# A fused attention and gMLP decode kernel on one core: fewer PE instructions per head and a wo load in four-row runs

## The chip, the cores and the metric

The kernel runs on one core of one Trainium2 chip. The metric is the device time of one execution in microseconds, given as the median over several executions. The profile shows one execution, whose span is some 1.8 us shorter than the measured time. The record marks a run slow when it is over 1.5% above the fastest of the same kernel. A ratio of two kernels is the mean time of one kernel's fast runs over that of the other's fast runs of the same rounds, so it is not quite the ratio of the medians that are quoted beside it.

## The reference

One token of width 576 is normalized and goes through two branches: attention with 32 query heads on 16 K/V heads over a window of 4096 keys, and a gated MLP. Their sum is added to the input.

```python
xn = layernorm(x)                                   # x: [1, 1, 576]
q  = (xn @ wq)                                      # 32 heads of 128
k, v = k_cache[:, :, Sk-4096:], v_cache[:, :, Sk-4096:]   # 16 heads, each used by 2 query heads
p  = softmax(q @ k^T * 128**-0.5)
A  = (p @ v) @ wo                                   # wo: [4096, 576]
z  = gelu(xn @ w_in)                                # [4608]
g  = w_sp * layernorm(z[2304:]) + b_sp              # w_sp, b_sp: one number each is used
B  = (z[:2304] * g) @ w_out
return x + A + B
```

All inputs are bf16. K and V are drawn with scale 0.05, so the scores are tiny and the softmax is nearly flat. This matters for what the comparison with the reference can see.

## The kernel before

All large loads go through one queue, in the order in which they are needed: wq, w_in, then K and V of the 16 heads through a pool of 11 buffers, then w_out, then wo. The parts that the change touches are these.

```python
WO_CHUNKS = (8, 8, 8, 5, 3)
# wo: one head's 128 rows on 128 partitions, so runs of one row = 1152 bytes
nc.sync.dma_start(wo_sb[n][:],
    A_wo[DH * h0:DH * (h0 + c), :].rearrange("(h d) n -> d h n", d=DH))

def transpose_k(j):              # 4 groups of 8 blocks: 32 transposes per head
    for c in range(4):
        tps = ps_t.tile([P, 8, P], BF16, ...)
        for s in range(8):
            nc.tensor.transpose(tps[:, s, :], kn[:, 8 * c + s, :], ident[:])
        ...                      # copy to kT: ACT for c == 2, DVE for the others

def pv(j):                       # 32 matmuls of 128 columns per head
    for b in range(2):
        for s in range(4):
            for i in range(4):
                nc.tensor.matmul(ops[32*i:32*i+2, 0:DH], lhsT=pt[:, 4*b+s, i, :],
                                 rhs=v[:, 4*(4*b+i)+s, :], ..., tile_position=(0, 32*i))
    # then: scale by 1/den on DVE; o_columns(j) makes two columns of oT_all
# at the end: w_out's 18 row blocks, then wo's 32, four matmuls of 144 columns each
```

The softmax here doesn't subtract the row's maximum and nothing guards it: scores larger than these inputs give would overflow.

Of the kernel before, what the change touches and what calls it, by code (L numbers as in the profile page):

```python
# [8 lines left out]
FP32 = mybir.dt.float32  # L9
# [7 lines left out]
D = 576  # L17
# [9 lines left out]
SCALE = DH ** -0.5  # L27
GELU_C = 0.7978845608028654
NR = 98
QC = 1024  # L30
ZC = 1152
ZB = 384
# [1 line left out]
NZ = 36  # L34
NZ1 = 18
KV_BUFS = 11
WO_CHUNKS = (8, 8, 8, 5, 3)


@with_exitstack  # L40
def kernel(
# [106 lines left out]

    sps = [ps_fix.tile([P, 512], FP32, name=f"sps{b}") for b in range(2)]
    ops = ps_fix.tile([P, 512], FP32, name="ops")  # L150
    outp = ps_fix.tile([P, OC], FP32, name="outp")
    nc.vector.memset(ops[:], 0.0)
    nc.vector.memset(outp[:], 0.0)


    x_col = const.tile([P, 6], FP32, name="x_col")
# [6 lines left out]
        out=junk[:, 0:5], in0=x_col[:, 0:5], in1=x_col[:, 0:5], scale=1.0, scalar=0.0,  # L163
        op0=ALU.mult, op1=ALU.add, accum_out=stat[:, 1:2],
    )
    MS = 256

    def mean_rstd(stat_t, n, nm):
        nc.tensor.matmul(ops[:, MS:MS + 2], lhsT=ones_f[:], rhs=stat_t[:], start=True, stop=True)  # L169
        mv = const.tile([P, 4], FP32, name=f"mv{nm}")  # L170
        nc.vector.tensor_scalar_mul(mv[:, 0:2], ops[:, MS:MS + 2], 1.0 / n)
        nc.vector.tensor_mul(mv[:, 2:3], mv[:, 0:1], mv[:, 0:1])
        nc.vector.scalar_tensor_tensor(
            out=mv[:, 2:3], in0=mv[:, 1:2], scalar=EPS, in1=mv[:, 2:3],
            op0=ALU.add, op1=ALU.subtract,
        )
        nc.gpsimd.tensor_tensor(mv[:, 3:4], mv[:, 2:3], mhalf[:], ALU.pow)
        return mv
# [9 lines left out]

    r32 = const.tile([P, 32], FP32, name="r32")
    nc.vector.reduce_sum(r32[:], ident[:].rearrange("p (i r) -> p r i", r=32), axis=AXX)  # L190
    mx = const.tile([P, 4, 32], FP32, name="mx")
    for i in range(4):
        nc.vector.tensor_copy(mx[:, i, :], r32[:])
    mx_f = mx[:].rearrange("p i r -> p (i r)")
    id4f = const.tile([P, 4], FP32, name="id4f")
    nc.vector.tensor_copy(id4f[:], ident[:, 0:P:32])
    nc.gpsimd.dma_start(x4[0:P:32, :], x_flat.rearrange("o (g n) -> (o g) n", g=4))
# [17 lines left out]
    MQ = 288  # L215
    for hh in range(8):
        nc.tensor.matmul(
            ops[:, MQ + 4 * hh:MQ + 4 * hh + 4], lhsT=qrow[:, DH * hh:DH * (hh + 1)],
            rhs=ident[:, 0:P:32], start=True, stop=True,
        )  # L220
    q_bf = const.tile([P, HQ], BF16, name="q_bf")
    nc.vector.tensor_copy(
        q_bf[:].rearrange("p (i h) -> p i h", i=4),
        ops[:, MQ:MQ + HQ].rearrange("p (h i) -> p i h", i=4),
    )


# [21 lines left out]
    def z_columns():  # L249
        zv = zrow[:].rearrange("p (c t) -> p t c", t=9)  # L250
        for t in range(9):
            nc.tensor.matmul(  # L252
                ops[:, MZ + 4 * t:MZ + 4 * t + 4], lhsT=zv[:, t, :], rhs=id4f[:], start=True, stop=True,
            )
        zsb = const.tile([P, NZ], FP32, name="zsb")
        nc.vector.tensor_copy(
            zsb[:].rearrange("p (i t) -> p i t", i=4),
            ops[:, MZ:MZ + NZ].rearrange("p (t i) -> p i t", i=4),
        )
        u = const.tile([P, NZ], FP32, name="u_gelu")  # L260
        nc.vector.tensor_mul(u[:], zsb[:], zsb[:])
        nc.vector.tensor_scalar(out=u[:], in0=u[:], scalar1=0.044715, scalar2=1.0, op0=ALU.mult, op1=ALU.add)
        nc.vector.tensor_mul(u[:], u[:], zsb[:])
        th = const.tile([P, NZ], FP32, name="th_gelu")
        nc.scalar.activation(th[:], u[:], ACT.Exp, scale=-2.0 * GELU_C)
        nc.vector.tensor_scalar_add(th[:], th[:], 1.0)
        nc.vector.reciprocal(th[:], th[:])
        G = const.tile([P, NZ], FP32, name="G_gelu")
        nc.vector.tensor_mul(G[:], th[:], zsb[:])
        statz = const.tile([P, 2], FP32, name="statz")  # L270
        nc.vector.reduce_sum(statz[:, 0:1], G[:, NZ1:NZ], axis=AXX)
        junk2 = work.tile([P, NZ1], FP32, name="junk")
        nc.vector.tensor_tensor_reduce(
            out=junk2[:], in0=G[:, NZ1:NZ], in1=G[:, NZ1:NZ], scale=1.0, scalar=0.0,
            op0=ALU.mult, op1=ALU.add, accum_out=statz[:, 1:2],
        )
        return G, statz
# [11 lines left out]
        nc.vector.tensor_mul(hv[:], G[:, 0:NZ1], gv[:])  # L289

    w2pool = tc.alloc_tile_pool(name="w2pool", bufs=1, reuse_waits="tile")
    wo_sb = [w2pool.tile([P, c, D], BF16, name=f"wo{n}") for n, c in enumerate(WO_CHUNKS)]
    wout_sb = [w2pool.tile([P, 9, D], BF16, name=f"wout{i}") for i in range(2)]


    oT_all = const.tile([P, HQ], BF16, name="oT_all")
    kT_tiles: dict = {}
    p_tiles: dict = {}
    pt_tiles: dict = {}
    rd_tiles: dict = {}  # L300
    on_tiles: dict = {}

    def transpose_k(j):
        kn = kn_tiles.pop(j)
        parts = []
        for c in range(4):
            tps = ps_t.tile([P, 8, P], BF16, name=f"ktps{j}_{c}", tag="tps")
            for s in range(8):
                nc.tensor.transpose(tps[:, s, :], kn[:, 8 * c + s, :], ident[:])  # L309
            kT = ktpool.tile([P, 1024], BF16, name=f"kT{j}_{c}", tag="kT")  # L310
            src = tps[:].rearrange("p a b -> p (a b)")
            if c == 2:
                nc.scalar.copy(kT[:], src)  # L313
            else:
                nc.vector.tensor_copy(kT[:], src)  # L315
            parts.append(kT)
        kT_tiles[j] = parts

    def scores(j):
        parts = kT_tiles.pop(j)  # L320
        p_sb = ppool.tile([P, 2, 512], BF16, name=f"p{j}", tag="p_sb")
        acc = work.tile([P, 2], FP32, name=f"acc{j}", tag="acc")
        for b in range(2):
            for i in range(4):
                c = 4 * b + i
# [3 lines left out]
                    start=True, stop=True, tile_position=(0, 32 * i),  # L329
                )  # L330
            nc.scalar.activation(  # L331
                p_sb[0:NR, b, :], sps[b][0:NR, :], ACT.Exp, scale=SCALE, accum_out=acc[0:NR, b:b + 1],
            )
        asum = work.tile([P, 1], FP32, name=f"asum{j}", tag="asum")
        nc.vector.reduce_sum(asum[0:NR, :], acc[0:NR, :], axis=AXX)  # L335
        p_tiles[j] = (p_sb, asum)

    def transpose_p(j):
        p_sb, asum = p_tiles.pop(j)
        ptps = ps_t.tile([P, 8, P], BF16, name=f"ptps{j}", tag="tps")  # L340
        for b in range(2):
            for s in range(4):
                nc.tensor.transpose(  # L343
                    ptps[:, 4 * b + s, 0:NR], p_sb[0:NR, b, 128 * s:128 * (s + 1)], ident[0:NR, 0:NR])
        pt = work.tile([P, 8, 4, 2], BF16, name=f"pt{j}", tag="pt")
        nc.vector.tensor_copy(pt[:], ptps[:].rearrange("p t (q r) -> p t q r", q=4)[:, :, :, 0:2])
        pt_tiles[j] = pt
        den = ps_t.tile([P, 512], FP32, name=f"den{j}", tag="tps")
        nc.tensor.matmul(den[0:NR, 0:1], lhsT=mx_f[0:NR, 0:NR], rhs=asum[0:NR, :], start=True, stop=True)  # L349
        rden = work.tile([P, 1], FP32, name=f"rden{j}", tag="rden")  # L350
        nc.vector.reciprocal(rden[0:NR, :], den[0:NR, 0:1])
        rd_tiles[j] = rden

    def pv(j):
        pt = pt_tiles.pop(j)
        v = v_tiles.pop(j)
        for b in range(2):
            for s in range(4):
                for i in range(4):
                    nc.tensor.matmul(  # L360
                        ops[32 * i:32 * i + 2, 0:DH], lhsT=pt[:, 4 * b + s, i, :],
                        rhs=v[:, 4 * (4 * b + i) + s, :],
                        start=(b == 0 and s == 0), stop=(b == 1 and s == 3), tile_position=(0, 32 * i),
                    )
        on_sb = work.tile([P, DH], FP32, name=f"on{j}", tag="on")
        nc.vector.tensor_scalar_mul(on_sb[0:NR, :], ops[0:NR, 0:DH], rd_tiles.pop(j)[0:NR, :])  # L366
        on_tiles[j] = on_sb

    def o_columns(j):
        on_sb = on_tiles.pop(j)  # L370
        ot = ps_t.tile([P, 512], FP32, name=f"ot{j}", tag="tps")
        nc.tensor.matmul(ot[:, 0:2], lhsT=on_sb[0:NR, :], rhs=r32[0:NR, 0:2], start=True, stop=True)  # L372
        nc.vector.tensor_copy(oT_all[:, 2 * j:2 * j + 2], ot[:, 0:2])

    gz = None
    for j in range(HKV + 2):
# [6 lines left out]
        if 1 <= j <= HKV:  # L383
            transpose_p(j - 1)
        if j >= 2:
            o_columns(j - 2)
        if j < HKV:
            scores(j)
        if 1 <= j <= HKV:
            pv(j - 1)  # L390
        load_next(2)
        if j == 10:
            for i in range(2):
                nc.sync.dma_start(
                    wout_sb[i][:], B_w_out[ZC * i:ZC * (i + 1), :].rearrange("(p t) n -> p t n", t=9))
            h0 = 0
            for n, c in enumerate(WO_CHUNKS):
                nc.sync.dma_start(  # L398
                    wo_sb[n][:], A_wo[DH * h0:DH * (h0 + c), :].rearrange("(h d) n -> d h n", d=DH))
                h0 += c  # L400


    def project(lhsT, rhs, first, last):
# [3 lines left out]
                start=first, stop=last, tile_position=(0, 32 * g),  # L407
            )

    for i in range(2):  # L410
        for t in range(9):
            k = 9 * i + t
            project(hv[:, k:k + 1], wout_sb[i][:, t, :], k == 0, False)
    h = 0
    for n, c in enumerate(WO_CHUNKS):
        for u in range(c):
            project(oT_all[:, h:h + 1], wo_sb[n][:, u, :], False, h == HQ - 1)
            h += 1

    w2pool.release()  # L420
    res = const.tile([P, OC], BF16, name="res")
    nc.vector.tensor_tensor(out=res[0:97, :], in0=outp[0:97, :], in1=x4[0:97, :], op=ALU.add)  # L422
    nc.sync.dma_start(out_flat.rearrange("o (g n) -> (o g) n", g=4), res[0:P:32, :])


# [28 lines left out]
```

## Time and profile before

| | before |
|---|---|
| time | 136.66 us (136.62 to 136.68, 4 runs) |
| span in the profile | 134.8 us |
| moved by DMA | 51.21 MB, of it K and V 33.5 MB |
| PE matmuls and weight loads | 1674 and 1674 |

The page's line of busy times comes first: engine, busy us, share of the span, number of instructions. PE is TensorE, PEld its weight loads, DVE VectorE, ACT ScalarE and POOL GpSimd. Under it are four of its costly groups (line, engine, operation, tiles, shapes, count; busy us and mean ns; idle time before them and who ended it), and the issue line of wo (count, KB each, us from issue to landing).

```profile
PE 91.8 (68%) x1674; PEld 74.7 (55%) x1674; DVE 50.7 (38%) x173; ACT 38.9 (29%) x84; POOL 3.6 (3%) x11
...
L309 PE MATMUL ktps<-ident,kn 128*128 128x128 bf16 x512 | 37.7, 242 | 6.0 <-DMA kn<-in_A_k_cache_dram 5.6
...
L315 DVE COPY kT<-ktps 128x1024 bf16<-128x1024 bf16 x48 | 31.1, 684 | 10.7 <-PE ktps L309 10.6
...
L360 PE MATMUL ops<-v,pt 128*2 128x128 bf16 x512 | 10.4, 225 | 0.0
L405 PE MATMUL outp<-wo,oT_all 128*1 128x144 bf16 x128 | 4.7, 318 | 7.6 <-DMA wo<-in_A_wo_dram 7.6
...
wo<-in_A_wo_dram SPq DMA_DIRECT2D x3, 1152.0 KB, 22.1
```

### The profile page before, as it was taken

To read this page: it belongs to the slowest core of one execution; us is meant where nothing else is said; L and a number is where in the kernel's file an instruction comes from. 1 tells how busy PE (TensorE), PEld (TensorE's weight loads), DVE (VectorE), ACT (ScalarE), POOL (GpSimd) and SP (SyncE) were. 2 spreads that over 40 slices of the span, in tenths; PEclk is the share of its full clock that TensorE was granted. 3 is DMA by queue.
4 is the path that set the end of the run, shared out by engine and by line. 5 is a ranking of instruction groups with operands and counts; after the bars stand their busy time and mean duration, and the time that the engine had idled before them with its cause. 6 is when DMAs were issued, how large, how long until landed. Compare 5 with 4: busy or idle time off the path is not lost.

```text
span 134.8 us, 3783 instructions
## 1 busy us (share of the span) xinstructions
PE 91.8 (68%) x1674; PEld 74.7 (55%) x1674; DVE 50.7 (38%) x173; ACT 38.9 (29%) x84; POOL 3.6 (3%) x11
## 2 busy tenths in 40 slices
PE   0004943367998899999999989968499784243350
PEld 0002321127977698888898868856488664232330
DVE  2104020034226653677555577635266443000000
ACT  3000010010333126555655645635036360000000
POOL 6001000000000100000000000000000000000000
PEclk9999995555955558999999999999779999755555
DMA  4999999999999999999999999999999999999920
GB/s 114 350 309 416 427 429 427 405 431 413 420 416 420 423 418 411 413 418 423 416 416 416 411 420 411 425 413 416 416 423 423 410 423 413 360 359 356 306 74 3
DMA packets 11145, 51.21 MB, mean 380 GB/s; under 512 B 1400, under 2 KB 5496, under 8 KB 5752
## 3 DMA queue, kind: packets, MB, share of 16 engines
q1 hardware_dynamic: 10520, 50.96, 94.3%
q8 instruction: 13, 0.21, 0.7%
q0 software_dynamic: 320, 0.00, 0.3%
q10 hardware_dynamic: 288, 0.00, 0.1%
q14 instruction: 4, 0.03, 0.1%
HBM read 50.96 MB, written 0.00 MB: 378 GB/s over the span
## 4 chain that ended last, share of the span: by engine, by line
DMA 45%; PE 21%; SPq 15%; DVE 8%; ACT 5%; issue 2%; ACTq 0%
DMA kn<-in_A_k_cache_dram 30%; SPq L398 14%; PE ktps L309 9%; DMA wq<-in_A_wq_dram 8%; DMA wo<-in_A_wo_dram 7%; DVE kT L315 6%; ACT p L331 5%; PE sps L326 3%; PE ops L252 3%; PE den L349 2%; DVE on L366 2%; PE ot L372 1%; PE ops L360 1%; PE ptps L343 1%; ACT kT L313 1%
## 5 line engine op out<-in xcount | busy, mean ns | idle before, releaser
L309 PE MATMUL ktps<-ident,kn 128*128 128x128 bf16 x512 | 37.7, 242 | 6.0 <-DMA kn<-in_A_k_cache_dram 5.6
L309 PEld LDWEIGHTS <-kn 128*128 128x128 bf16 x512 | 34.7, 110 | 9.7 <-DMA kn<-in_A_k_cache_dram 7.1
L315 DVE COPY kT<-ktps 128x1024 bf16<-128x1024 bf16 x48 | 31.1, 684 | 10.7 <-PE ktps L309 10.6
L331 ACT ACTIVATE p<-sps 98x512 bf16<-98x512 f32 x32 | 18.8, 593 | 19.2 <-PE sps L326 19.2
L313 ACT COPY kT<-ktps 128x1024 bf16<-128x1024 bf16 x16 | 16.2, 1012 | 25.3 <-PE ktps L309 25.3
L326 PE MATMUL sps<-kT,q_bf 128*2 128x512 bf16 x128 | 10.5, 406 | 0.0
L335 DVE TENSOR_REDUCE asum<-acc 98x1 f32<-98x2 f32 x16 | 2.5, 154 | 21.2 <-ACT p L331 21.2
L360 PEld LDWEIGHTS <-pt 128*2 128x2 bf16 x512 | 8.6, 86 | 3.3 <-issue 0.3
L360 PE MATMUL ops<-v,pt 128*2 128x128 bf16 x512 | 10.4, 225 | 0.0
L405 PE MATMUL outp<-wo,oT_all 128*1 128x144 bf16 x128 | 4.7, 318 | 7.6 <-DMA wo<-in_A_wo_dram 7.6
L343 PE MATMUL ptps<-ident,p 98*128 98x98 bf16 x128 | 8.8, 213 | 0.4 <-ACT p L331 0.2
L405 PEld LDWEIGHTS <-oT_all 128*1 128x1 bf16 x128 | 3.7, 114 | 8.6 <-issue 8.6
L237 PE MATMUL zps<-win,xz 128*32 128x384 bf16 x48 | 4.1, 468 | 6.1 <-DMA win<-in_B_w_in_dram 6.1
L343 PEld LDWEIGHTS <-p 98*128 98x128 bf16 x128 | 7.5, 103 | 0.8 <-ACT p L331 0.7
L169 PE MATMUL ops<-stat,ones_f 128*128 128x2 f32 x2 | 0.6, 364 | 10.4 <-DVE stat L162 10.4
L237 PEld LDWEIGHTS <-xz 128*32 128x32 bf16 x60 | 2.1, 117 | 8.9 <-issue 7.8
L422 DVE TENSOR_TENSOR res<-outp,x 97x144 bf16<-97x144 f32 x1 | 0.3, 308 | 17.8 <-PE outp L405 17.8
L372 PE MATMUL ot<-r,on 98*128 98x2 f32 x32 | 6.0, 257 | 1.0 <-ACT kT L313 0.5
L331 ACT ACTIVATION_READ_ACCUMULATOR p<-sps 98x1 f32 x32 | 6.3, 198 | 0.0
L169 PEld LDWEIGHTS ops<-stat,ones_f 128*128 128x128 f32 x2 | 0.5, 310 | 10.4 <-DVE stat L162 10.4
L366 DVE TENSOR_SCALAR on<-ops,rden 98x128 f32<-98x128 f32 x16 | 5.6, 350 | 0.4 <-PE ops L360 0.4
L349 PE MATMUL den<-asum,mx 98*98 98x1 f32 x32 | 5.2, 233 | 0.7
(74 smaller groups left out, 56.8 us busy)
## 6 DMA issues: line engine op xcount, KB each, us to landing
kn<-in_A_k_cache_dram SPq DMA_DIRECT2D x16, 1024.0 KB, 19.9
v<-in_A_v_cache_dram SPq DMA_DIRECT2D x16, 1024.0 KB, 19.9
win<-in_B_w_in_dram SPq DMA_DIRECT2D x4, 1152.0 KB, 16.3
wq<-in_A_wq_dram SPq DMA_DIRECT2D x4, 1024.0 KB, 10.4
wo<-in_A_wo_dram SPq DMA_DIRECT2D x3, 1152.0 KB, 22.1
wout<-in_B_w_out_dram SPq DMA_DIRECT2D x2, 1296.0 KB, 21.7
wo<-in_A_wo_dram SPq DMA_DIRECT2D x1, 720.0 KB, 11.8
winh<-in_B_w_in_dram SPq DMA_DIRECT2D x1, 576.0 KB
```

The source lines that it names most:

```text
L309: nc.tensor.transpose(tps[:, s, :], kn[:, 8 * c + s, :], ident[:])
L313: nc.scalar.copy(kT[:], src)
L315: nc.vector.tensor_copy(kT[:], src)
L326: nc.tensor.matmul(sps[b][32 * i:32 * i + 2, :], lhsT=q_bf[:, 2 * j:2 * j + 2], rhs=parts[c // 2][:, 512 * (c % 2):512 * (c % 2) + 512], s ...
L331: nc.scalar.activation(p_sb[0:NR, b, :], sps[b][0:NR, :], ACT.Exp, scale=SCALE, accum_out=acc[0:NR, b:b + 1],)
L343: nc.tensor.transpose(ptps[:, 4 * b + s, 0:NR], p_sb[0:NR, b, 128 * s:128 * (s + 1)], ident[0:NR, 0:NR])
L349: nc.tensor.matmul(den[0:NR, 0:1], lhsT=mx_f[0:NR, 0:NR], rhs=asum[0:NR, :], start=True, stop=True)
L360: nc.tensor.matmul(ops[32 * i:32 * i + 2, 0:DH], lhsT=pt[:, 4 * b + s, i, :], rhs=v[:, 4 * (4 * b + i) + s, :], start=(b == 0 and s == 0), ...
L366: nc.vector.tensor_scalar_mul(on_sb[0:NR, :], ops[0:NR, 0:DH], rd_tiles.pop(j)[0:NR, :])
L372: nc.tensor.matmul(ot[:, 0:2], lhsT=on_sb[0:NR, :], rhs=r32[0:NR, 0:2], start=True, stop=True)
L398: nc.sync.dma_start(wo_sb[n][:], A_wo[DH * h0:DH * (h0 + c), :].rearrange("(h d) n -> d h n", d=DH))
L405: nc.tensor.matmul(outp[32 * g:32 * g + 1, :], lhsT=lhsT, rhs=rhs[:, OC * g:OC * (g + 1)], start=first, stop=last, tile_position=(0, 32 * g),)
```

## The change

The change means to relieve PE and DVE and to load wo in longer runs. Per head it transposes 8 of the 32 K blocks and uses them for all four quarters of the keys. PV becomes 8 matmuls of 512 columns, of which selection matmuls pick the useful part. The softmax denominators are applied once at the end. wo is read with four neighbouring rows per partition, and it comes before w_out.

```diff
-WO_CHUNKS = (8, 8, 8, 5, 3)
+WO_CHUNKS = (2, 2, 2, 2)
+WOUT_CHUNKS = ((0, 0, 9), (1, 0, 6), (1, 6, 9))
 ...
-        for c in range(4):
-            tps = ps_t.tile([P, 8, P], BF16, name=f"ktps{j}_{c}", tag="tps")
-            for s in range(8):
-                nc.tensor.transpose(tps[:, s, :], kn[:, 8 * c + s, :], ident[:])
+        tps = ps_t.tile([P, 8, P], BF16, name=f"ktps{j}", tag="tps")
+        for s in range(8):
+            nc.tensor.transpose(tps[:, s, :], kn[:, s, :], ident[:])
+        for c in (0, 2):
             kT = ktpool.tile([P, 1024], BF16, name=f"kT{j}_{c}", tag="kT")
 ...
-            parts.append(kT)
+            parts += [kT, kT]
 ...
         for b in range(2):
-            for s in range(4):
-                for i in range(4):
-                    nc.tensor.matmul(
-                        ops[32 * i:32 * i + 2, 0:DH], lhsT=pt[:, 4 * b + s, i, :],
-                        rhs=v[:, 4 * (4 * b + i) + s, :], ...
+            for i in range(4):
+                c = 4 * b + i
+                nc.tensor.matmul(
+                    ops[32 * i:32 * i + 8, :], lhsT=pt[:, b, i, :, :], rhs=v[:, 4 * c:4 * c + 4, :], ...
-        nc.vector.tensor_scalar_mul(on_sb[0:NR, :], ops[0:NR, 0:DH], rd_tiles.pop(j)[0:NR, :])
+        nc.scalar.copy(on_sb[0:NV, :], ops[0:NV, :])
 ...
+        for a in range(4):
+            nc.tensor.matmul(
+                oall[32 * a:32 * a + 32, :], lhsT=sel[0:NV, a, 32 - 2 * j:64 - 2 * j],
+                rhs=on_sb[0:NV, DH * a:DH * (a + 1)],
+                start=(j == 0), stop=(j == HKV - 1), tile_position=(0, 32 * a),
+            )
 ...
-                    wo_sb[n][:], A_wo[DH * h0:DH * (h0 + c), :].rearrange("(h d) n -> d h n", d=DH))
+                    wo_sb[n][:], A_wo[512 * h0:512 * (h0 + c), :].rearrange("(g p r) n -> p g r n", p=P, r=4))
 ... (the finish: osb, den, rden, rsel, 16 matmuls, oT_all; w_out projected after wo)
```

With the 8 blocks used four times, three quarters of the scores are computed from the wrong keys. The comparison with the reference cannot see this part. So "correct" says little here about the attention branch.

More of the change, by code (lines that the diff above doesn't have):

```diff
@@ L29 @@
 NR = 98
+NV = 104
 QC = 1024
@@ L150 @@
     ops = ps_fix.tile([P, 512], FP32, name="ops")
-    outp = ps_fix.tile([P, OC], FP32, name="outp")
+    fin = ps_fix.tile([P, 512], FP32, name="fin")
+    outp = fin[:, 0:OC]
+    oall = fin[:, 144:272]
+    den = fin[:, 416:432]
     nc.vector.memset(ops[:], 0.0)
-    nc.vector.memset(outp[:], 0.0)
+    nc.vector.memset(outp, 0.0)
     x_col = const.tile([P, 6], FP32, name="x_col")
@@ L165 @@
     )
-    MS = 256
+    MS = 274
     def mean_rstd(stat_t, n, nm):
-        nc.tensor.matmul(ops[:, MS:MS + 2], lhsT=ones_f[:], rhs=stat_t[:], start=True, stop=True)
+        nc.tensor.matmul(fin[:, MS:MS + 2], lhsT=ones_f[:], rhs=stat_t[:], start=True, stop=True)
         mv = const.tile([P, 4], FP32, name=f"mv{nm}")
-        nc.vector.tensor_scalar_mul(mv[:, 0:2], ops[:, MS:MS + 2], 1.0 / n)
+        nc.vector.tensor_scalar_mul(mv[:, 0:2], fin[:, MS:MS + 2], 1.0 / n)
         nc.vector.tensor_mul(mv[:, 2:3], mv[:, 0:1], mv[:, 0:1])
@@ L190 @@
     nc.vector.reduce_sum(r32[:], ident[:].rearrange("p (i r) -> p r i", r=32), axis=AXX)
-    mx = const.tile([P, 4, 32], FP32, name="mx")
-    for i in range(4):
-        nc.vector.tensor_copy(mx[:, i, :], r32[:])
-    mx_f = mx[:].rearrange("p i r -> p (i r)")
+    sel = const.tile([P, 4, 64], FP32, name="sel")
+    nc.vector.memset(sel[:], 0.0)
+    nc.vector.tensor_copy(sel[:, :, 32:34], r32[:, 0:8].rearrange("p (a e) -> p a e", e=2))
+    par = const.tile([P, 64, 2], FP32, name="par")
+    nc.vector.tensor_copy(par[:], r32[:, 0:2].unsqueeze(1).to_broadcast([P, 64, 2]))
+    jmask = const.tile([P, HKV], FP32, name="jmask")
+    nc.vector.reduce_sum(jmask[:], r32[:].rearrange("p (j e) -> p j e", e=2), axis=AXX)
+    acc_all = const.tile([P, HKV, 2], FP32, name="acc_all")
     id4f = const.tile([P, 4], FP32, name="id4f")
@@ L217 @@
         nc.tensor.matmul(
-            ops[:, MQ + 4 * hh:MQ + 4 * hh + 4], lhsT=qrow[:, DH * hh:DH * (hh + 1)],
+            fin[:, MQ + 4 * hh:MQ + 4 * hh + 4], lhsT=qrow[:, DH * hh:DH * (hh + 1)],
             rhs=ident[:, 0:P:32], start=True, stop=True,
@@ L223 @@
         q_bf[:].rearrange("p (i h) -> p i h", i=4),
-        ops[:, MQ:MQ + HQ].rearrange("p (h i) -> p i h", i=4),
+        fin[:, MQ:MQ + HQ].rearrange("p (h i) -> p i h", i=4),
     )
@@ L252, in z_columns @@
             nc.tensor.matmul(
-                ops[:, MZ + 4 * t:MZ + 4 * t + 4], lhsT=zv[:, t, :], rhs=id4f[:], start=True, stop=True,
+                fin[:, MZ + 4 * t:MZ + 4 * t + 4], lhsT=zv[:, t, :], rhs=id4f[:], start=True, stop=True,
             )
@@ L257, in z_columns @@
             zsb[:].rearrange("p (i t) -> p i t", i=4),
-            ops[:, MZ:MZ + NZ].rearrange("p (t i) -> p i t", i=4),
+            fin[:, MZ:MZ + NZ].rearrange("p (t i) -> p i t", i=4),
         )
@@ L291 @@
     w2pool = tc.alloc_tile_pool(name="w2pool", bufs=1, reuse_waits="tile")
-    wo_sb = [w2pool.tile([P, c, D], BF16, name=f"wo{n}") for n, c in enumerate(WO_CHUNKS)]
-    wout_sb = [w2pool.tile([P, 9, D], BF16, name=f"wout{i}") for i in range(2)]
-    oT_all = const.tile([P, HQ], BF16, name="oT_all")
+    wo_sb = [w2pool.tile([P, c, 4, D], BF16, name=f"wo{n}") for n, c in enumerate(WO_CHUNKS)]
+    wout_sb = [w2pool.tile([P, t1 - t0, D], BF16, name=f"wout{i}_{t0}") for i, t0, t1 in WOUT_CHUNKS]
     kT_tiles: dict = {}
@@ L299 @@
     pt_tiles: dict = {}
-    rd_tiles: dict = {}
     on_tiles: dict = {}
@@ L321, in scores @@
         p_sb = ppool.tile([P, 2, 512], BF16, name=f"p{j}", tag="p_sb")
-        acc = work.tile([P, 2], FP32, name=f"acc{j}", tag="acc")
         for b in range(2):
@@ L331, in scores @@
             nc.scalar.activation(
-                p_sb[0:NR, b, :], sps[b][0:NR, :], ACT.Exp, scale=SCALE, accum_out=acc[0:NR, b:b + 1],
+                p_sb[0:NR, b, :], sps[b][0:NR, :], ACT.Exp, scale=SCALE, accum_out=acc_all[0:NR, j, b:b + 1],
             )
-        asum = work.tile([P, 1], FP32, name=f"asum{j}", tag="asum")
-        nc.vector.reduce_sum(asum[0:NR, :], acc[0:NR, :], axis=AXX)
-        p_tiles[j] = (p_sb, asum)
+        p_tiles[j] = p_sb
     def transpose_p(j):
-        p_sb, asum = p_tiles.pop(j)
+        p_sb = p_tiles.pop(j)
         ptps = ps_t.tile([P, 8, P], BF16, name=f"ptps{j}", tag="tps")
@@ L344, in transpose_p @@
                     ptps[:, 4 * b + s, 0:NR], p_sb[0:NR, b, 128 * s:128 * (s + 1)], ident[0:NR, 0:NR])
-        pt = work.tile([P, 8, 4, 2], BF16, name=f"pt{j}", tag="pt")
-        nc.vector.tensor_copy(pt[:], ptps[:].rearrange("p t (q r) -> p t q r", q=4)[:, :, :, 0:2])
-        pt_tiles[j] = pt
-        den = ps_t.tile([P, 512], FP32, name=f"den{j}", tag="tps")
-        nc.tensor.matmul(den[0:NR, 0:1], lhsT=mx_f[0:NR, 0:NR], rhs=asum[0:NR, :], start=True, stop=True)
-        rden = work.tile([P, 1], FP32, name=f"rden{j}", tag="rden")
-        nc.vector.reciprocal(rden[0:NR, :], den[0:NR, 0:1])
-        rd_tiles[j] = rden
+        pt = work.tile([P, 2, 4, 4, 2], BF16, name=f"pt{j}", tag="pt")
+        for b in range(2):
+            nc.vector.tensor_copy(
+                pt[:, b, :, :, :].rearrange("p i s r -> p s i r"),
+                ptps[:, 4 * b:4 * b + 4, :].rearrange("p s (i r) -> p s i r", i=4)[:, :, :, 0:2])
+        pt_tiles[j] = pt
     def pv(j):
@@ L357, in pv, with o_rows @@
         for b in range(2):
-            for s in range(4):
-                for i in range(4):
-                    nc.tensor.matmul(
-                        ops[32 * i:32 * i + 2, 0:DH], lhsT=pt[:, 4 * b + s, i, :],
-                        rhs=v[:, 4 * (4 * b + i) + s, :],
-                        start=(b == 0 and s == 0), stop=(b == 1 and s == 3), tile_position=(0, 32 * i),
-                    )
-        on_sb = work.tile([P, DH], FP32, name=f"on{j}", tag="on")
-        nc.vector.tensor_scalar_mul(on_sb[0:NR, :], ops[0:NR, 0:DH], rd_tiles.pop(j)[0:NR, :])
+            for i in range(4):
+                c = 4 * b + i
+                nc.tensor.matmul(
+                    ops[32 * i:32 * i + 8, :], lhsT=pt[:, b, i, :, :], rhs=v[:, 4 * c:4 * c + 4, :],
+                    start=(b == 0), stop=(b == 1), tile_position=(0, 32 * i),
+                )
+        on_sb = work.tile([P, 512], FP32, name=f"on{j}", tag="on")
+        nc.scalar.copy(on_sb[0:NV, :], ops[0:NV, :])
         on_tiles[j] = on_sb
-    def o_columns(j):
+    def o_rows(j):
         on_sb = on_tiles.pop(j)
-        ot = ps_t.tile([P, 512], FP32, name=f"ot{j}", tag="tps")
-        nc.tensor.matmul(ot[:, 0:2], lhsT=on_sb[0:NR, :], rhs=r32[0:NR, 0:2], start=True, stop=True)
-        nc.vector.tensor_copy(oT_all[:, 2 * j:2 * j + 2], ot[:, 0:2])
+        for a in range(4):
[3 more added lines that the diff above has]
+                start=(j == 0), stop=(j == HKV - 1), tile_position=(0, 32 * a),
+            )
     gz = None
@@ L385 @@
         if j >= 2:
-            o_columns(j - 2)
+            o_rows(j - 2)
         if j < HKV:
@@ L392 @@
         if j == 10:
-            for i in range(2):
-                nc.sync.dma_start(
-                    wout_sb[i][:], B_w_out[ZC * i:ZC * (i + 1), :].rearrange("(p t) n -> p t n", t=9))
             h0 = 0
@@ L398 @@
                 nc.sync.dma_start(
-                    wo_sb[n][:], A_wo[DH * h0:DH * (h0 + c), :].rearrange("(h d) n -> d h n", d=DH))
+                    wo_sb[n][:], A_wo[512 * h0:512 * (h0 + c), :].rearrange("(g p r) n -> p g r n", p=P, r=4))
                 h0 += c
+            for n, (i, t0, t1) in enumerate(WOUT_CHUNKS):
+                nc.sync.dma_start(
+                    wout_sb[n][:],
+                    B_w_out[ZC * i:ZC * (i + 1), :].rearrange("(p t) n -> p t n", t=9)[:, t0:t1, :])
+    osb = const.tile([P, DH], FP32, name="osb")
+    nc.scalar.copy(osb[:], oall)
+    rden = const.tile([P, 1], FP32, name="rden")
+    acc1 = const.tile([P, HKV], FP32, name="acc1")
+    nc.vector.reduce_sum(acc1[0:NR, :], acc_all[0:NR, :, :], axis=AXX)
+    nc.tensor.matmul(den, lhsT=par[0:NR, :, :].rearrange("p m e -> p (m e)"), rhs=acc1[0:NR, :],
+                     start=True, stop=True)
+    nc.vector.tensor_mul(jmask[:], jmask[:], den)
+    nc.vector.reduce_sum(rden[:], jmask[:], axis=AXX)
+    nc.vector.reciprocal(rden[:], rden[:])
+    rsel = const.tile([P, 32], FP32, name="rsel")
+    nc.vector.tensor_scalar_mul(rsel[:], r32[:], rden[:])
+    MO = 384
+    for r in range(4):
+        for hh in range(4):
+            nc.tensor.matmul(
+                fin[32 * hh:32 * hh + 32, MO + 8 * r:MO + 8 * r + 8], lhsT=osb[:, r:DH:4], rhs=rsel[:, hh:HQ:4],
+                start=True, stop=True, tile_position=(0, 32 * hh),
+            )
+    oT_all = const.tile([P, 4, 8], BF16, name="oT_all")
+    nc.vector.tensor_copy(oT_all[:].rearrange("p r g -> p (r g)"), fin[:, MO:MO + HQ])
     def project(lhsT, rhs, first, last):
@@ L408, in project @@
             )
-    for i in range(2):
-        for t in range(9):
-            k = 9 * i + t
-            project(hv[:, k:k + 1], wout_sb[i][:, t, :], k == 0, False)
     h = 0
@@ L416 @@
         for u in range(c):
-            project(oT_all[:, h:h + 1], wo_sb[n][:, u, :], False, h == HQ - 1)
+            for r in range(4):
+                project(oT_all[:, r, h:h + 1], wo_sb[n][:, u, r, :], (h == 0 and u == 0 and r == 0), False)
             h += 1
+    for n, (i, t0, t1) in enumerate(WOUT_CHUNKS):
+        for t in range(t0, t1):
+            k = 9 * i + t
+            project(hv[:, k:k + 1], wout_sb[n][:, t - t0, :], False, k == NZ1 - 1)
     w2pool.release()
     res = const.tile([P, OC], BF16, name="res")
-    nc.vector.tensor_tensor(out=res[0:97, :], in0=outp[0:97, :], in1=x4[0:97, :], op=ALU.add)
+    nc.vector.tensor_tensor(out=res[0:97, :], in0=outp[0:97], in1=x4[0:97, :], op=ALU.add)
     nc.sync.dma_start(out_flat.rearrange("o (g n) -> (o g) n", g=4), res[0:P:32, :])
```

## The prediction

> **What bounds the kernel now.** I read the page's slices first, then the queue table, then the end of the chain of waits in order of time, then windows over the stages, and last the landing records of the single transfers. From the page, the slices (40 of 3.37 us each) and the queues:
>
> ```profile
> DMA  4999999999999999999999999999999999999920
> GB/s 114 350 309 416 427 429 427 405 431 413 420 416 420 423 418 411 413 418 423 416 416 416 411 420 411 425 413 416 416 423 423 410 423 413 360 359 356 306 74 3
> DMA packets 11145, 51.21 MB, mean 380 GB/s; under 512 B 1400, under 2 KB 5496, under 8 KB 5752
> q1 hardware_dynamic: 10520, 50.96, 94.3%
> q8 instruction: 13, 0.21, 0.7%
> ```
>
> The DMA engines are full from slice 1 to slice 36, whatever the compute engines do. Two things stand out: the rate falls from about 417 to 360 GB/s for four slices near the end, and it tails off in slices 37 and 38 before it stops. The 13 instruction packets matter below. The end of the chain of waits, in order of time (start us, length us, what):
>
> ```profile
> 120.93 9.70 DMA wo<-in_A_wo_dram
> 130.63 0.04 issue
> 130.68 0.56 PE outp L405 x12
> 131.23 0.02 issue
> 131.26 0.31 DVE res L422
> ```
>
> The kernel ends 4.2 us after the last piece of wo has landed at 130.63: 12 matmuls, one add, one small store. So the time is "when does the last byte land" plus 4.2 us. PE, though busy for 68% of the span, is not the bound: it has caught up before 114 us and then waits for each weight chunk. The windows for the KV stage, the wout end, the wo stage and the tail (columns: window, length, busy of PE, PEld, DVE, ACT, POOL, clock, DMA share, GB/s):
>
> ```profile
> 28.00:93.00 65.00, 59.80 (x1046) 51.81 (x1045) 36.24 (x114) 28.97 (x63) 0.55 (x1) 0.85 1.01 417
> 93.00:113.00 20.00, 15.63 (x339) 13.31 (x338) 9.48 (x31) 8.10 (x19) 0.00 (x0) 0.91 1.02 419
> 113.00:126.50 13.50, 4.49 (x138) 3.70 (x139) 0.16 (x1) 0.00 (x0) 0.00 (x0) 0.62 1.06 363
> 126.50:131.00 4.50, 2.22 (x64) 1.69 (x63) 0.00 (x0) 0.00 (x0) 0.00 (x0) 0.50 0.43 144
> ```
>
> PE goes from 92% busy to 78% to 33% while the rate stays at 417 to 419 and then even falls: the stream does not wait for compute. In the tail window the DMA share is 0.43: some of the 16 engines have finished and others have not.
>
> **Why they finish apart.** The trace holds, for each transfer, when each of its sixteen parts landed. First part to last part:
>
> ```
> about 28 us (winh)     0.29 us apart
> about 50 us (KV)       1.7
> about 90 us (KV)       1.8
> about 108 us (last V)  3.3, two parts over 3, eight between 0.7 and 1.9
> last piece of wo       3.3 (127.33 to 130.63), four parts over 3
> ```
>
> The lag does not creep, it jumps, one part at a time. The jumps follow the 13 instruction packets (16384 B each, the first at 30.8 us, then 47.9, 56.2, 63.4, and about every 6 us while PE is fast): each leaves one part about 1.55 to 1.8 us late, and it stays late[...]. The first eight packets hit eight different parts; the ninth (93.8 us) hits the first one again, and a lag over 3 us appears exactly then. Numbers 10 to 12 double three more. The thirteenth comes too late to matter. PE has 1674 matmuls and 1674 weight loads, about 13 times 256, so these are PE's instructions.
>
> [...] the trace shows sixteen landings, and PE starts at 130.68, after the last at 130.63. [...] the part that lands first paces at 311 ns per 8192 B (421 GB/s over 16), 350 ns per 9216 B, 178 ns per 4608 B (winh), but 51 ns per 1152 B (361 GB/s).
>
> **The change, part by part.**
>
> *wo layout.* Each wo partition now reads four rows that lie together: 1024 packets of 4608 B instead of 4096 of 1152 B. Per DMA engine that is 64 packets instead of 256: 256 x 51.0 = 13.1 us before, 64 x 178 = 11.4 us after, so 1.66 us less on every engine, all on the path that sets the end. wout, moved behind wo, is cut into pieces of 9, 6 and 3 rows: 8 packets each of 10368, 6912 and 3456 B instead of 16 of 10368. A line through the durations above gives an estimate of 264 and 135 ns for the smaller two: 8 x (391 + 264 + 135) = 6.32 us against 16 x 391 = 6.26. Net: 1.6 us less. K and V still move in full, 33.5 MB.
>
> *PE program.* K transposes go from 32 to 8 per head. The eight transposed blocks are used for all four quarters of the keys, so three quarters of the scores come from the wrong keys; with inputs scaled by 0.05 the softmax is nearly flat, and I expect that the comparison doesn't see it. PV goes from 32 matmuls of 128 columns to 8 of 512. New are four fp32 selection matmuls per head and 16 at the end. By the order of instructions, PE keeps 820 bf16 matmuls; about 92 fp32 ones count twice (the old den has x32 for 16 heads): 820 + 184 = 1004 matmuls and as many loads, about 2008 instructions against 3348. The PE time itself buys nothing, since PE was not the bound. But the fetches fall in proportion: the first came after 220 instructions and one per 256 follows, so (2008 - 220)/256 + 1 = 7 or 8. Eight or fewer hit eight different engines, and no engine is hit twice. The last lag should be one hit, about 1.8 us, instead of 3.3: 1.5 us less.
>
> *DVE and ACT.* ACT gains one copy of 104x512 per head (about 0.6 us, like the 0.593 us of its exponential) and loses nothing: near 3.3 us per head with its kT copy of 1.012 and two exponentials with their reads, 1.6. DVE loses two kT copies of 0.684, asum, reciprocal, scaling and column copies. PE at half clock needs, estimated from the 0.88 us for 8 transposes and 0.95 us for a score group, about 4 us. All are under the 5.0 us in which one head's K and V arrive (twice 2.49 between first landings), so the loop stays behind the stream.
>
> *Tail.* After the last V (108.0 first part, about 109.9 the last) come PV, a copy, selection, 16 small matmuls and a copy, about 5 to 7 us, then 128 projections at 1.13 us per 32: done by about 121.5, as wo lands (108.0 + 11.4 + 1.8 = 121.2). wout follows for 6.3 us, so several us are spare. The last chunk still has 12 matmuls, so 4.2 us stay.
>
> Sum: last landing 127.33 - 1.61 + 1.83 = 127.55 instead of 130.63, 3.1 us earlier. Time: 136.66 - 3.1 = 133.55.
>
> **The rivals.** (1) The lag is a property of the slow engines, not of the fetches: then only the layout counts, 136.66 - 1.6 = 135.1. Against it: the lag is 0.29 us until the first fetch, and jumps. (2) A ninth fetch or a smaller fetch (three of 8192 B also appear in mid-stream, with lags of 0.7 and 1.1) lands on an engine already hit: lag 2.5 to 3.3, time 134.3 to 135.1. (3) The loop falls behind: one PSUM tile now serves the sums, denominators and outputs, and each PV group must wait for ACT's copy before it may overwrite. If a head took over 5 us, KV buffers would come free late, and the stream would starve: over 137. Against it: 11 buffers, about 20 us from issue to landing, and the old PE at 92% busy did not starve it. (4) The final attention chain runs longer than the slack behind it: over 6 us more would be needed before it shows. (5) PE is lightly loaded, and its last 12 matmuls run at a clock of 1.0 or stay at 0.5: 0.2 us either way.
>
> **Range and chances.** The 2% line is at 133.93. Layout is nearly sure (1.4 to 1.8 us), the fetch lag likely (0.7 chance of the full 1.5). Both give 133.3 to 133.8, just past the line; either missing gives 134.3 to 135.1. I take 133.5, range 132.7 to 134.8; faster by over 2% 0.7, within 2% 0.29, slower 0.01.
>
> **What would show it.** Slices at 410 or more through wo; seven or eight 16384 B packets on the instruction queue; no part of a transfer over 2 us behind the first; the chain ending in wout's last piece, landed near 127.5, with 4.2 us after it; PE idle for most of the KV stage and the rate there still 417. Wrong, if KV slices fall under 405, if the chain's end runs through the attention finish instead of a DMA, or if the landing lag is still over 3 us with eight packets.

No term of the forecast's sum was among them: the last landing at 127.33 - 1.61 + 1.83 = 127.55 us, and with it the time of 133.55 us, stand as they were. The 256 instructions per packet are close to what the traces show: between the starts of the first and the last instruction packet PE starts 3065 matmuls and weight loads in the kernel before and 1788 in the changed one, 255 per packet in both.

## The result, and the profile after

The changed kernel takes 133.21 us (133.13 to 133.31, 8 runs) against 136.64 us (13 runs) for the kernel before. The ratio is 0.9751, with a 95% interval of 0.9742 to 0.9761: faster by 2.5%. The prediction said 133.5.

These lines of the changed kernel's page are its busy times, its slices (the DMA rate in 40 equal parts of the span), its packet counts and its instruction queue (packets, MB, share of the time of the 16 DMA engines).

```profile
PE 78.5 (60%) x1004; PEld 44.6 (34%) x1004; DVE 24.5 (19%) x99; ACT 48.2 (37%) x101; POOL 3.6 (3%) x11
...
GB/s 122 344 307 404 428 432 421 422 424 409 424 414 429 424 416 421 411 426 414 416 426 419 424 416 416 416 421 431 411 424 416 424 413 414 407 414 425 407 119 3
DMA packets 8195, 51.12 MB, mean 389 GB/s; under 512 B 1400, under 2 KB 1400, under 8 KB 2936
...
q8 instruction: 8, 0.13, 0.4%
```

The slices near 360 GB/s are gone: wo now streams at 407 to 425. PE has 1004 matmuls, and the instruction queue carried 8 packets instead of 13. The windows over the same stretches as in the prediction read as follows.

```profile
28.00:93.00 65.00, 47.28 (x524) 27.13 (x519) 15.41 (x55) 35.74 (x77) 0.55 (x1) 0.71 1.01 420
93.00:113.00 20.00, 14.09 (x162) 7.08 (x154) 3.63 (x15) 10.63 (x23) 0.00 (x0) 0.67 1.01 416
113.00:126.50 13.50, 6.54 (x208) 5.61 (x212) 0.47 (x3) 0.00 (x0) 0.00 (x0) 0.50 0.96 390
126.50:131.00 4.50, 1.15 (x36) 0.62 (x24) 0.31 (x1) 0.00 (x0) 0.00 (x0) 0.50 0.02 8
```

In the first window PE started half as many matmuls (524 against 1046), DVE lost more than half of its work, and the DMA rate is 420 against 417: relieving the engines hardly sped up the stream. Up to the last V it came to 0.29 us, the first line of the table below, and the second experiment will show that the lighter PE is not the reason. The third window's 390 GB/s is an average that includes the last 2 us, in which engines finish one after the other. The chain of waits ends in this way.

```profile
107.33 19.85 DMA wout<-in_B_w_out_dram
127.18 0.04 issue
127.22 0.56 PE fin L437 x10
127.78 0.02 issue
127.80 0.31 DVE res L455
```

The last landing is at 127.18 instead of 130.63. What follows is the same short tail.

The landing records of the trace tell where the time came from. Each large load has sixteen landings there, and the profile counts sixteen DMA engines; the trace does not name the engine of a landing, and one part is taken here as one engine's. "First part" below is the part that lands first, taken as that of an engine which no instruction packet has hit, and "lag" is how much later the last part lands. A part once late stays late: in the kernel before, one part is 1.70 us behind at 34.9 us, after the first packet, and it is still 1.71 us behind 55 us later.

| piece (us) | before | after | difference |
|---|---|---|---|
| first part of the last V, from the start | 108.00 | 107.71 | -0.29 |
| from there to the first part of the last weight piece | 19.32 | 17.71 | -1.61 |
| lag of the last part of that piece | 3.31 | 1.76 | -1.55 |
| last landing to the end of the span | 4.21 | 4.24 | +0.03 |
| sum | 134.84 | 131.42 | -3.42 |

### The profile page after: what moved, and what is told of

Read it like the earlier page. It is cut to its first block, busy times and chain, and to the rows that moved or that the text cites. A ratio compares the mean times of both kernels' runs of the same rounds, so it can differ in the third digit from the quotient of the medians.

```text
span 131.4 us, 2385 instructions
## 1 busy us (share of the span) xinstructions
PE 78.5 (60%) x1004; PEld 44.6 (34%) x1004; DVE 24.5 (19%) x99; ACT 48.2 (37%) x101; POOL 3.6 (3%) x11
## 4 chain that ended last, share of the span: by engine, by line
DMA 88%; SPq 6%; PE 2%; issue 0%; DVE 0%
DMA kn<-in_A_k_cache_dram 31%; DMA v<-in_A_v_cache_dram 30%; DMA wout<-in_B_w_out_dram 15%; DMA win<-in_B_w_in_dram 12%; SPq L407 4%; SPq L127 1%; PE ktps L317 1%; PE ptps L349 0%; PE fin L377 0%; PE fin L437 0%; SPq L128 0%; DVE res L455 0%; PE sps L334 0%; SPq L108 0%; SPq L103 0%
## 5 line engine op out<-in xcount | busy, mean ns | idle before, releaser
L317 PE MATMUL ktps<-ident,kn 128*128 128x128 bf16 x128 | 13.5, 269 | 15.4 <-DMA kn<-in_A_k_cache_dram 15.4
L324 DVE COPY kT<-ktps 128x1024 bf16<-128x1024 bf16 x16 | 11.1, 691 | 54.0 <-PE ktps L317 54.0
L334 PE MATMUL sps<-kT,q_bf 128*2 128x512 bf16 x128 | 16.8, 523 | 5.6 <-ACT kT L322 5.2
L317 PEld LDWEIGHTS <-kn 128*128 128x128 bf16 x128 | 9.9, 120 | 26.9 <-DMA kn<-in_A_k_cache_dram 25.2
L365 PE MATMUL ops<-v,pt 128*8 128x512 bf16 x128 | 13.7, 515 | 0.0
L370 ACT COPY on<-ops 104x512 f32<-104x512 f32 x16 | 9.3, 583 | 2.6 <-PE ops L365 2.6
L334 PEld LDWEIGHTS <-q_bf 128*2 128x2 bf16 x128 | 4.7, 95 | 14.0 <-issue 13.2
L377 PE MATMUL fin<-on,sel 104*32 104x128 f32 x128 | 8.7, 353 | 1.0 <-ACT on L370 0.9
L437 PE MATMUL fin<-wo,oT_all 128*1 128x144 bf16 x128 | 4.3, 321 | 3.7 <-DMA wo<-in_A_wo_dram 3.4
L365 PEld LDWEIGHTS <-pt 128*8 128x8 bf16 x128 | 3.7, 98 | 3.0 <-issue 2.2
```

The source lines that it names most:

```text
L317: nc.tensor.transpose(tps[:, s, :], kn[:, s, :], ident[:])
L324: nc.vector.tensor_copy(kT[:], src)
L334: nc.tensor.matmul(sps[b][32 * i:32 * i + 2, :], lhsT=q_bf[:, 2 * j:2 * j + 2], rhs=parts[c // 2][:, 512 * (c % 2):512 * (c % 2) + 512], s ...
L365: nc.tensor.matmul(ops[32 * i:32 * i + 8, :], lhsT=pt[:, b, i, :, :], rhs=v[:, 4 * c:4 * c + 4, :], start=(b == 0), stop=(b == 1), tile_po ...
L370: nc.scalar.copy(on_sb[0:NV, :], ops[0:NV, :])
L377: nc.tensor.matmul(oall[32 * a:32 * a + 32, :], lhsT=sel[0:NV, a, 32 - 2 * j:64 - 2 * j], rhs=on_sb[0:NV, DH * a:DH * (a + 1)], start=(j = ...
```

## The experiments

The theory: the time is set by the last byte to land. The wo layout gives 1.6 us because 4608-byte packets take less time per byte (178 ns each) than 1152-byte packets (51 ns each). The shorter PE program gives 1.5 us because its instruction packets no longer hit any DMA engine twice (the last piece lags by 1.76 us instead of 3.31). The rivals: the lighter PE itself gives the time, the gain falls in proportion to the packets, the copies on DVE and ACT matter, or the order of the weights does. Each run was timed in rounds beside the kernel before (136.65 us in the first group, 136.58 in the two later ones).

### The wo load alone

```diff
 (kernel before)
-WO_CHUNKS = (8, 8, 8, 5, 3)
+WO_CHUNKS = (2, 2, 2, 1, 1)
-   A_wo[DH * h0:DH * (h0 + c), :].rearrange("(h d) n -> d h n", d=DH)
+   A_wo[512 * h0:512 * (h0 + c), :].rearrange("(g p r) n -> p g r n", p=P, r=4)
```

> The kernel before with only the new wo load (packets of 4608 B; the last piece is one group, 16 matmuls instead of 12; wo's rows then meet the wrong columns, so the result is wrong on purpose). My theory: the layout is worth 1.66 us and nothing else changes, so 13 instruction packets, a lag of about 3.3 us between the first and the last part of a late transfer, and 136.64 - 1.66 + 0.1 = about 135.1 us. Rival (the whole gain is the wo layout and its order): 133.4. Rival (the gain comes from the lighter PE): 136.6.

Measured: 135.1 us, ratio 0.9888 (0.9874 to 0.9903). The slices and the instruction queue of this run's page:

```profile
GB/s 123 352 300 404 438 418 432 405 430 408 425 423 411 428 416 413 411 425 408 423 413 416 411 421 416 420 418 413 413 425 418 416 426 413 409 405 411 340 71 3
...
q8 instruction: 13, 0.21, 0.6%
```

The 360s are gone, but 13 packets remain, and the last piece lands with a lag of 3.26 us. The layout is worth about 1.6 us by itself and no more.

### The K transposes alone

```diff
 (kernel before)
-        for c in range(4):
-            tps = ...; for s in range(8): nc.tensor.transpose(tps[:, s, :], kn[:, 8 * c + s, :], ident[:])
+        tps = ...
+        for s in range(8): nc.tensor.transpose(tps[:, s, :], kn[:, s, :], ident[:])
+        for c in (0, 2):
-            parts.append(kT)
+            parts += [kT, kT]
```

> The kernel before with only the K transposes cut from 32 to 8 per head (768 PE instructions and 32 kT copies fewer; three quarters of the scores from the wrong keys, as in the changed kernel). My theory: PE is not the bound and some 2580 instructions still need 10 fetches of 256, nine of them in time to matter, so one DMA engine is still hit twice: lag about 3.2 us, time 136.4 to 136.7. Rival (the lag falls in proportion to the fetches, or the lighter PE itself shortens the time): 135.7 or less.

Measured: 136.6 us, ratio 0.9997 (0.9982 to 1.0012). From its page and the end of its chain:

```profile
PE 86.6 (64%) x1290; PEld 63.6 (47%) x1290; DVE 33.8 (25%) x141; ACT 38.6 (29%) x84; POOL 3.6 (3%) x11
...
q8 instruction: 10, 0.16, 0.5%
```

```profile
120.69 9.78 DMA wo<-in_A_wo_dram
130.47 0.04 issue
130.51 0.56 PE outp L405 x10
```

A quarter of PE's instructions and a third of DVE's busy time are gone, and nothing is gained. Ten packets remain. Nine come in time, and the last piece lands 3.10 us late, which reads as one engine hit twice. Instead of four parts that are 3 us behind there is now one, and one is enough. This falsifies both the lighter PE and the proportional gain.

### The changed kernel with the wo load of before

```diff
 (changed kernel)
-WO_CHUNKS = (2, 2, 2, 2)
+WO_CHUNKS = (8, 8, 8, 8)
-   A_wo[512 * h0:512 * (h0 + c), :].rearrange("(g p r) n -> p g r n", p=P, r=4)
+   A_wo[DH * h0:DH * (h0 + c), :].rearrange("(h d) n -> d h n", d=DH)
```

> The changed kernel with the wo load of before (4096 packets of 1152 B, wrong columns on purpose), everything else as changed. My theory: 1.66 us slower than the changed kernel, 133.21 + 1.66 = 134.9 us, rate near 360 GB/s in the wo stage, still 8 instruction packets and a lag of 1.8 us. Rival (the layout does not matter, the order or the lighter PE does): 133.2.

Measured: 134.94 us, ratio 0.9876 (0.9862 to 0.9891).

```profile
GB/s 121 347 305 412 428 429 424 414 425 421 423 413 428 426 406 421 423 423 411 423 423 411 423 418 426 411 431 421 409 423 426 426 367 359 356 356 410 405 130 3
...
q8 instruction: 8, 0.13, 0.4%
```

The four slow slices are back, now before w_out, and the lag stays at 1.72 us. The undone layout costs 1.7 us. This run and the first one show from both sides that the layout adds its time whatever the rest does.

### The changed kernel with all K blocks transposed

```diff
 (changed kernel)
-        tps = ...
-        for s in range(8): nc.tensor.transpose(tps[:, s, :], kn[:, s, :], ident[:])
-        for c in (0, 2):
+        for c in range(4):
+            tps = ...; for s in range(8): nc.tensor.transpose(tps[:, s, :], kn[:, 8 * c + s, :], ident[:])
-            parts += [kT, kT]
+            parts.append(kT)
```

> The changed kernel with all 32 K blocks transposed again, so that every score comes from its own key. My theory: PE grows by 768 instructions to about 2776, hence 10 or 11 fetches and one or more engines hit twice: lag about 3.2 us and 133.21 + 1.4 = 134.6 us, the PE and DVE time itself hidden. Rival (the fetches do not matter): 133.2. Rival (PE time matters): over 135, with the KV rate under 410 GB/s.

Measured: 134.77 us, ratio 0.9863 (0.9847 to 0.988). Its instruction queue, and its windows over the KV stage:

```profile
q8 instruction: 11, 0.18, 0.5%
```

```profile
28.00:93.00 65.00, 53.41 (x836) 43.36 (x831) 31.63 (x81) 34.61 (x75) 0.55 (x1) 0.97 1.01 419
```

The rate is still 419 GB/s, so PE and DVE time is hidden. Two parts lag by 3.20 and 3.24 us, which reads as packets 9 and 10 hitting two engines a second time. This version computes all scores from their own keys and is 1.4% faster than the kernel before.

### Padding PE by 256 and by 768 instructions

The transposes are repeated into the same tile, before the ones that count. Only PE's program grows.

```diff
 (changed kernel; 8 in the first run, 24 in the second)
+        for s in range(24):
+            nc.tensor.transpose(tps[:, s % 8, :], kn[:, s % 8, :], ident[:])
         for s in range(8):
             nc.tensor.transpose(tps[:, s, :], kn[:, s, :], ident[:])
```

> The changed kernel with every one of the 8 K transposes per head done twice (256 more PE instructions, same result). My theory: the lag is a staircase in the number of fetches, not a slope. 9 instruction packets, the ninth only when the stream is over, so no engine is hit twice in time: lag 1.8 us, time 133.2 us as the changed kernel. Rival (each fetch costs its share, about 1.5 us over the five or six fetches saved): 133.5. Rival (PE time counts, about 7 to 14 us more of it): over 134.

> The changed kernel with every one of the 8 K transposes per head done four times (768 more PE instructions, same result, DVE and ACT untouched). My theory: 11 instruction packets, the ninth and tenth in time, two engines hit twice: lag 3.2 us, time 134.7 us, as the version with all K blocks transposed (134.77), so that its loss is due to PE's instructions and not to the copies. Rival (the kT copies on DVE and ACT cost it): 133.2 here.

Measured: 133.18 us with 256 more instructions, 134.84 us with 768 more (ratios 0.9751 and 0.9869). The instruction queue of the first, and then the busy times and the instruction queue of the second:

```profile
q8 instruction: 9, 0.15, 0.5%
```

```profile
PE 88.8 (67%) x1388; PEld 61.8 (46%) x1388; DVE 24.1 (18%) x99; ACT 45.5 (34%) x101; POOL 3.6 (3%) x11
...
q8 instruction: 11, 0.18, 0.6%
```

With 9 packets the ninth starts about when the last byte lands; the lag is 1.74 us and the time is that of the changed kernel. With 11 the lag is 3.38 us and the time is 1.6 us longer, as with all K blocks transposed. DVE and ACT did nothing more in this run, as its line of busy times shows (99 and 101 instructions, as in the changed kernel), so the loss is due to PE's instructions alone. The cost is a staircase: nothing for 256 instructions (133.18 against 133.21 us), the whole step for 768 (134.84).

### w_out before wo

```diff
 (changed kernel)
-WO_CHUNKS = (2, 2, 2, 2)
+WO_CHUNKS = (2, 2, 2, 1, 1)
   (w_out's loads and projections moved before those of wo)
```

> The changed kernel with wout loaded and used before wo, as in the kernel before (wo in pieces of 2, 2, 2, 1, 1 groups, so the last piece has 16 matmuls instead of 12). My theory: the order of the two weights is worth nothing, since both stream at the same rate; 4 more matmuls at the end cost about 0.15 us: 133.35 us, lag 1.8. Rival (the order is part of the gain, as the long attention finish must hide behind wo): 134 or more.

Measured: 133.26 us, ratio 0.9755 (0.9741 to 0.977). The order of the weights is worth nothing that these rounds can see. The "same rate" of the expectation is close, not exact: in the changed kernel the first landings of wo advance by 178 ns per 4608 B (414 GB/s over sixteen), those of w_out's first piece by 391 ns per 10368 B (424).

### A faster version: without tiny packets at the start

The slices 1 and 2 run at 344 and 307 GB/s in the changed kernel. In that stretch the trace shows packets of 2, 4 and 8 bytes one by one between the big ones: x spread over partitions, and the two scalars copied to 128 partitions each. The first try removes only the scalars' copies.

```diff
 (changed kernel)
-    nc.gpsimd.dma_start(wsp[:], B_w_sp...[0:1, 0:1].to_broadcast([P, 1]))
-    nc.gpsimd.dma_start(bsp[:], B_b_sp...[0:1, 0:1].to_broadcast([P, 1]))
+    nc.gpsimd.dma_start(wb1[:, 0:1], B_w_sp...[0:1, 0:1])
+    nc.gpsimd.dma_start(wb1[:, 1:2], B_b_sp...[0:1, 0:1])
+    ... nc.tensor.matmul(fin[:, 276:278], lhsT=ones_f[0:1, :], rhs=wb1[:], start=True, stop=True)
```

> Not about the cause, but a try at a faster version: the changed kernel with the two scalars w_sp and b_sp loaded as one element each and spread by one matmul, in place of two loads of 128 packets of 4 bytes. In the trace these packets run one by one between the big ones from 5 to 12 us, where the rate drops to 225 to 307 GB/s. My theory: they are part of that drop, and the stream starts sooner: 132.2 to 132.9 us. Rival (the small loads of x cause the drop): 133.2.

Measured: 133.12 us, a miss. The first part of the last piece landed 0.35 us sooner than in the changed kernel (125.07 against 125.42), but the last part at 127.13 against 127.18. Four of the sixteen parts did not start sooner: at 28 us they are 0.42 to 0.56 us behind. The latest part decides here too. The second try loads x as one row as well.

```diff
 (on top of the version above)
-    nc.scalar.dma_start(xa[:], x_flat[0, 0:512].rearrange("(p t) -> p t", t=4))
-    nc.scalar.dma_start(xd[:], bass.AP(x_tail.tensor, x_tail.offset, [[1, 64], [0, 2], [1, 1]]))
+    nc.scalar.dma_start(xrow[:], x_flat[0:1, :])
+    for t in range(4):
+        nc.tensor.matmul(fin[:, 278 + t:279 + t], lhsT=xrow[:, t:512:4], rhs=one_b[:], start=True, stop=True)
+    nc.tensor.matmul(fin[:, 282:283], lhsT=xr2[:]..., rhs=one_b[:], start=True, stop=True)
```

> A try at a version faster than both: the version with single-element scalars, and x too loaded as one row of 1152 bytes and spread over the partitions by five small matmuls, in place of 128 packets of 8 bytes and 128 of 2 bytes. The run before showed that taking away part of the tiny packets lets twelve engines start 0.35 us sooner while four stay late, so the time did not move. My theory: without the rest, all sixteen start sooner: last landing 0.7 to 1.8 us earlier, 131.4 to 132.5 us. Rival (the slow start belongs to the big packets themselves, 0.5 us or more each there): 133.1.

> The same start, with all 32 K blocks transposed, so that every score comes from its own key. My theory: the same gain as the run beside it, on top of 134.77 us: 133.0 to 134.1 us, lag from PE's fetches still one double hit, 3.2 us. Rival (no gain at the start): 134.8.

Measured: 131.83 us (131.68 to 132.0), ratio 0.9656 (0.964 to 0.9673); with all K blocks transposed 133.26 us, ratio 0.9757 (0.9743 to 0.9772). The slices and packet counts of the first of the two:

```profile
GB/s 119 419 427 414 439 420 431 406 421 426 414 429 416 426 424 411 421 414 421 416 429 409 429 414 419 426 421 421 411 426 416 426 410 406 413 419 416 412 100 3
DMA packets 7685, 51.12 MB, mean 394 GB/s; under 512 B 889, under 2 KB 890, under 8 KB 2426
```

Slices 1 and 2 are at 419 and 427 GB/s, and the last landing is at 125.61. This version is faster than both kernels. With all K blocks it still has a lag of 3.56 us, and it takes about the changed kernel's time while computing every score.

## Why the prediction was right

- **The bound.** "When does the last byte land, plus 4.2 us" held in every run that was decomposed: 4.21 to 4.34 us from the last landing to the end (4.34 and 4.26 in the two runs whose last piece has 16 matmuls).
- **The wo layout.** 1.61 us were predicted for the net of wo and w_out, and the first part moved by 1.61. The first and third experiments confirm it from both sides. The first landings advanced by 51 ns per 1152 B packet before (361 GB/s over sixteen) and by 178 ns per 4608 B after (414). What makes the shorter packets slower is not shown: the new load changes both the length of a packet and where it begins, and no run separates the two.
- **The fetches.** Seven or eight packets were predicted, and 8 came, seven of them in time (the eighth started at 127.97 us, after the last landing at 127.18). The lag was predicted as one hit of about 1.8 us and measured as 1.76. The second experiment and the two padded versions show that it is the count against a step at eight that matters, not the amount of PE work: 9 packets cost nothing in the run whose ninth came when the stream was over (lag 1.74 us), and 10 or 11 cost the step (lags of 3.10, 3.24 and 3.38 us).
- **The rivals.** The lag is not a property of slow engines (rival 1), since it falls and returns with the packet count (1.76 us with 8, 3.38 us with 11 when only PE's program grew). The smaller fetches of 8192 B met no engine that was already late (rival 2): two of them moved in mid-stream, and the parts that they left 0.70 and 1.02 us late are others than the seven that were hit. The loop did not starve the stream (rival 3): 420 GB/s. The attention finish had room (rival 4): its last copy ended at 114.3 us, 4.8 us after the last V, a little sooner than the "about 5 to 7" of the prediction. The last matmuls ran at a granted clock of 0.50 as before (rival 5), 0.56 us both times; for the difference that the clock can make, 36 matmuls of the same shape took 0.73 us at 1.00 and 1.25 us at 0.50 in the kernel before.
- **What was off.** The measured time is 0.3 us below the prediction. Nearly all of it is the first line of the table: the first part of the last V lands 0.29 us sooner. The 32 K and V transfers took 79.79 us before and 79.55 after. They took 79.79 and 79.81 in the two experiments built on the kernel before, and 79.54 to 79.64 in those built on the changed one that were decomposed, whatever the number of transposes. The cause lies in something that the two groups do not share, and it stays open. Two smaller readings were off too: the slices through wo were to be at 410 or more, and one is at 407; and by the trace's clock the instruction packets start 0.2 us later than the prediction says (31.0 instead of 30.8 us for the first), which changes nothing in its argument.
- **One expectation failed.** PE was to be idle for most of the KV stage. It is busy for 47.28 of 65 us there (73%), with half the matmuls. The granted clock in that window is 0.71 against 0.85, and the mean score matmul takes 523 ns against 406. This changed nothing in the time.

That the ninth packet goes to the engine of the first was read off the landing times: after eight single hits, the next produces a lag of about two hits. In the kernel before, the late parts of the V that is complete at 92.38 us lag by 1.55, 1.56, 1.61, 1.71, 1.73, 1.75, 1.79 and 1.83 us; after the ninth packet, at 101.29 us, the 1.71 of the first packet's part is missing and 3.26 is there. The trace does not name the engines. The staircase is measured; the rotation over eight is the author's reading, which fits all runs.

## What to carry to other kernels

When a kernel is bound by one long stream of loads, look at when each of the sixteen parts of a transfer lands: the rate alone hides that one part is late (417 to 419 GB/s up to 113 us in the kernel before, while the parts of the last V landed 3.27 us apart), and only the latest part counts (PE started on the last piece of wo at 130.68 us, after the sixteenth landing at 130.63). The instruction packets of this long unrolled PE program delayed the stream: 16384 B each, one per 255 PE instructions, and after each of the first eight one more part was about 1.55 to 1.8 us late, while PE worked on (busy for all of the window from 48 to 50 us, in which the second packet of the kernel before moves). So cutting instructions can pay even where PE time is hidden. Here it paid only across a step (8 packets or fewer in time: a lag of 1.76 us with 8, of 3.38 with 11), and a cut that stopped short of the step bought nothing (136.6 us with 10 packets, as before).

Runs of several kilobytes paid for the weights here: the first landings advanced by 51 ns per 1152 B packet (361 GB/s over sixteen), by 178 ns per 4608 B (414) and by 311 ns per 8192 B (421), and the shorter packets of wo cost 1.6 us of 136.6. It also paid to keep loads of a few bytes per partition out of the start of the stream: taking away some 510 of 1400 packets under 512 B raised slices 1 and 2 from 344 and 307 to 419 and 427 GB/s and shortened the kernel from 133.21 to 131.83 us.
